# K's transposing load by rows of one key, and a score matmul that reads with a step of four

## The chip, the cores and the metric

The kernel runs on one core of one Trainium2 chip. The metric is the device time of one execution in microseconds. The five engines of a core work from their own instruction streams and meet at semaphores: TensorE (PE) multiplies matrices into PSUM, VectorE (DVE), ScalarE (ACT) and GpSimd (POOL) work element by element, and SyncE (SP) issues most of the transfers, which run on 16 DMA engines.

## The reference

Two problems, A and B, of the same sizes are computed independently; their outputs are joined on the last axis. Each is attention against a given cache, between a query and an output projection:

```
B, Sq, D = 16, 80, 576;  Hq, Hkv, Sk, Dh = 32, 16, 512, 128      (bfloat16)
q = (x @ wq).reshape(B, Sq, Hq, Dh).transpose(0, 2, 1, 3)
k, v = k_cache, v_cache, each of the 16 heads used by two query heads
scores = einsum("bhqd,bhkd->bhqk", q, k) * Dh ** -0.5
p = softmax(scores)
o = einsum("bhqk,bhkd->bhqd", p, v)
out = o.transpose(0, 2, 1, 3).reshape(B, Sq, Hq * Dh) @ wo
```

k_cache and v_cache have the shape (16, 16, 512, 128): for one batch row, four heads of K are 2048 keys of 128 numbers, 512 KB that lie in one piece in HBM.

## The kernel before

**Units.** The work is cut into 128 units, 64 of each problem. A unit is one batch row and four K/V heads (a "quad"), with the eight query heads that use them. Each K/V head has 2 x 80 = 160 query rows. 128 of them make one score tile; the 32 left over of each of the four heads are put together in one further tile of 128 rows. So a unit has five score tiles of 128 rows by 512 keys.

**K's load** (`em_ldk`, line 612) is a DMA transpose issued by SP. It brings the unit's 2048 keys into `kT`, with the 128 numbers of a key across the 128 partitions. `kT` has five buffers (`NK`), each of 4 x 512 elements per partition. The source is seen as 512 rows of four consecutive keys, "(g p) j d" with j = 4; in `kT` an element stands at [d, j, g*128 + p]. So `kT[:, ks, j, :]` holds, for each of the four heads, every fourth key.

**V's load** (`em_ldv`, line 616) is a plain DMA that puts four consecutive keys of a head into one partition: partition p has keys 4p to 4p + 3. That is why a score tile must have its columns in the order "j, then p": the four blocks of 128 columns, transposed, then meet the right rows of V.

**Scores.** `em_qk` (line 658) makes the tile of one head by one matmul: the head's queries are the stationary operand, 128 x 128, and K the moving one, `kT[:, ks, :, gl*128:(gl+1)*128]`, four runs of 128 elements, 512 columns in all. `em_qkr` (line 644) makes the left-over tile by four narrow matmuls with 32 query rows each, at the column tiles 0, 32, 64 and 96 of the array; from the third unit on, two units are done in one call, so eight matmuls stand together.

**After the scores**, for each tile: DVE takes the negated maximum (line 667), ACT the exponential with the row sum (line 671), DVE the reciprocal (line 677), POOL multiplies (line 680), PE transposes the tile in four blocks (line 686) and DVE copies them to `pT` (lines 692 and 694). In 45 of the units the left-over tile is transposed by a DMA from SP instead (line 698). Four matmuls for each head multiply with V (line 731); ACT copies the result to `oT` (line 747).

**Projections.** The query projection (line 540, in pieces of 480 and 160 columns) and the output projection (line 781, 288 columns) are spread between the units' work on PE. Query results are moved by ACT or DVE (lines 551 and 552); outputs are stored by SP (line 815). For problem B, x is brought in by four transposing loads: line 481 (640 rows of four blocks of 128 elements) and line 485 (640 rows of one such block).

**The order of the work.** A planner in Python (`_Sched`) gets every operation with a due time, an estimated duration and its resources, and writes out one fixed order for each engine; PSUM banks are given out there too. Score tiles are due 10 tiles before the rest of their unit (`LA`), K's load a further 8 (`KK`). The planner's costs for a K load (`dur=3.4` on SP, `cost=KC` on the DMA) are constants. Each engine runs its list strictly in order, with waits on semaphores; a K load waits until PE has done the score matmuls that read the same buffer five units before, and everything after it on SP waits with it.

Of the kernel before, what the change touches and what calls it, by code (L numbers as in the profile page):

```python
# [73 lines left out]
def _mm(n, cols):  # L74
    return n * (cols * MM1 + MM0)
# [248 lines left out]
def bass_concat_heads__gqa_block_cached__gqa_block_cached__near_ridge_kernel(  # L324
# [27 lines left out]
    with ExitStack() as es:  # L352
# [6 lines left out]
        kT = sb("kT", [128, NK, 4, 512], BF16)  # L359
# [24 lines left out]
        def R(res, ver):  # L384
            return (res, ver)
# [47 lines left out]
        def unit(g):  # L433
            prob, r = divmod(g, NOCT * NPP)
            pair, r = divmod(r, 2 * NPP)
            half, q = divmod(r, 2)
            return prob, 2 * pair + q, half
# [57 lines left out]
        for goct in range(NG):  # L495
            prob, q, half = unit(goct)
# [106 lines left out]
        for U in range(NSU):  # L603
            goct, bl = divmod(U, 8)
            prob, q, half = unit(goct)
            b = half * 8 + bl
            _, kc_ap, vc_ap, _, _ = probs[prob]
            ks, vs, pts, qsl = U % NK, U % NV, U % NPT, goct % NQ

            def em_ldk(e, kc_ap=kc_ap, b=b, q=q, ks=ks):  # L610
                src = kc_ap[b, 4 * q:4 * q + 4, :, :].rearrange("g (p j) d -> (g p) j d", j=4)
                return e.dma_start_transpose(kT[:, ks, :, :], src)

            def em_ldv(e, vc_ap=vc_ap, b=b, q=q, vs=vs):
                src = vc_ap[b, 4 * q:4 * q + 4, :, :].rearrange("g (p j) d -> p g (j d)", j=4)
                return e.dma_start(v_sb[:, vs, :, :], src)

            S.add("sp", 5.0 * gfirst[U] + 0.5 * (U - gfirst[U]) - LA - KK, em_ldk, writes=[R(("kT", ks), U)],
                  dsem="d_k%d" % ks, name="ldk%d" % U, stream="K", dur=3.4, cost=KC)
            S.add("sp", 5.0 * U - VK, em_ldv, writes=[R(("V", vs), U)],  # L620
# [4 lines left out]
            for k in range(5):  # L625
# [5 lines left out]
                gl = k - 1  # L631
# [5 lines left out]
                if k == 0:  # L637
                    group.append((U, vb, ks, qsl, bl, goct))
                    if len(group) == gsize[U]:
                        def em_qkr(e, group=tuple(group)):  # L640
                            last = None
                            for _, vb_, ks_, qsl_, bl_, _ in group:
                                for g4 in range(4):
                                    last = e.matmul(ps[32 * g4:32 * g4 + 32, vb_.phys, :],  # L644
                                                    lhsT=qT[:, qsl_, bl_, g4 * 160 + 128:g4 * 160 + 160],
                                                    rhs=kT[:, ks_, :, g4 * 128:(g4 + 1) * 128],
                                                    start=True, stop=True, tile_position=(0, 32 * g4))
                            return last

                        S.add("pe", Qof[(group[0][0], 0)] - LA + 0.0, em_qkr,  # L650
                              reads=[R(("qT", g_[3], g_[4], i), g_[5]) for g_ in group for i in (1, 3, 5, 7)]
                              + [R(("kT", g_[2]), g_[0]) for g_ in group],
                              writes=[R(g_[1], 0) for g_ in group], name="qkr%d" % U, stream="S",
                              dur=len(group) * (_mm(1, 512) + 0.0105), lat=0.2, alloc=[g_[1] for g_ in group], mode=1)
                        group = []
                else:
                    def em_qk(e, gl=gl, vb=vb, ks=ks, qsl=qsl, bl=bl):
                        return e.matmul(ps[:, vb.phys, :], lhsT=qT[:, qsl, bl, gl * 160:gl * 160 + 128],  # L658
                                        rhs=kT[:, ks, :, gl * 128:(gl + 1) * 128], start=True, stop=True)

                    S.add("pe", tq, em_qk,
                          reads=[R(("qT", qsl, bl, 2 * gl), goct), R(("qT", qsl, bl, 2 * gl + 1), goct),
                                 R(("kT", ks), U)],
                          writes=[R(vb, 0)], name="qk%d" % T, stream="S", dur=_mm(1, 512), lat=0.2, alloc=[vb])
# [230 lines left out]
```

## Time and profile before

| | |
|---|---|
| time, median of 3 runs | 781.7 us (779.27 to 785.27) |
| profiled execution: time / span | 780.9 us / 779.2 us |
| granted TensorE clock | 1.00 |
| busy: PE / DVE / ACT / POOL | 99% / 87% / 78% / 55% |
| DMA: moved, mean rate | 166.44 MB, 214 GB/s |
| DMA packets, of them under 512 B | 386,564, 300,576 |
| K load, time from issue to landing (min/median/max) | 4.3 / 6.0 / 10.6 us |

The profile comes from one execution. The span is the time from the first to the last instruction. "Busy" is the time in which an engine had an instruction running; matmuls are pipelined and their ends are modelled, so PE's busy share is no measure of how fast it works, and the spacing of two matmuls in the chain is more telling than the duration of one. L612 means line 612 of the kernel. "PEld" is the loading of stationary operands, "SPq" the instruction queue of SP. In the lists of waits each line has the waiting engine and line, what it waited for, the total in us, the number of times and the longest. The chain is followed back from the last instruction: at each step to what released it or, if nothing did, to the instruction before it on its engine.

### The profile page before, as it was taken

What the parts mean: (1) busy time and instruction counts of PE and PEld (TensorE: products, weight loads), DVE (VectorE), ACT (ScalarE), POOL (GpSimd) and SP (SyncE); (2) the same over time, 40 slices, a digit from 0 to 9 for tenths busy, and PEclk for the clock granted to TensorE, in tenths of its full rate; (3) what the DMA queues carried; (4) which work ended last, traced back from release to release, by engine and by line L of the source; (5) the groups of instructions that cost most, each with busy time, mean ns of one, the idle gap of its engine ahead of it and who ended that gap; (6) DMA issues with size and microseconds to landing.
All of it is one profiled execution on the core that took longest, in us unless ns stands there. A gap on an engine that the chain in (4) does not pass through costs nothing.

```text
span 779.2 us, 21256 instructions
## 1 busy us (share of the span) xinstructions
PE 772.0 (99%) x8078; PEld 567.5 (73%) x8078; DVE 678.6 (87%) x1558; ACT 611.6 (78%) x1736; POOL 432.4 (55%) x647
## 2 busy tenths in 40 slices
PE   9999999999999999999999999999999999999998
PEld 5576677777777777767777777777777777777786
DVE  4999988888888899888898899988888888989982
ACT  1878988888888888867787777978888887887860
POOL 1555755565655656555655655655655655664660
PEclk9999999999999999999999999999999999999999
DMA  9999999988899999999999999999999978999951
GB/s 249 226 259 240 249 222 247 203 188 197 205 200 213 204 237 247 251 213 227 211 229 214 177 214 244 258 218 237 221 230 202 200 177 196 257 220 210 187 134 32
DMA packets 386564, 166.44 MB, mean 214 GB/s; under 512 B 300576, under 2 KB 383008, under 8 KB 386464
## 3 DMA queue, kind: packets, MB, share of 16 engines
q1 hardware_dynamic: 385248, 163.91, 95.7%
q8 instruction: 65, 1.06, 0.6%
q10 hardware_dynamic: 1216, 1.18, 0.5%
q14 instruction: 35, 0.29, 0.1%
HBM read 87.46 MB, written 2.95 MB: 116 GB/s over the span
## 4 chain that ended last, share of the span: by engine, by line
PE 91%; DVE 7%; DMA 1%; ACT 0%; POOL 0%; issue 0%; SPq 0%
PE ps L540 20%; PE ps L781 20%; PE ps L731 17%; PE ps L686 15%; PE ps L658 13%; DVE negmax L667 4%; PE ps L644 4%; DVE pT L694 2%; DVE qT L552 1%; DMA kT<-in_A_k_cache_dram 1%; PE ps L409 0%; PE ps L464 0%; DVE pT L692 0%; ACT p_sb L671 0%; PE ps L424 0%; POOL p_sb L680 0%
## 5 line engine op out<-in xcount | busy, mean ns | idle before, releaser
L680 POOL TENSOR_SCALAR p_sb<-p_sb,rinv 128x512 bf16<-128x512 bf16 x640 | 430.0, 692 | 325.5 <-DVE rinv L677 325.1
L671 ACT ACTIVATE p_sb<-ps,negmax 128x512 bf16<-128x512 f32 x640 | 441.3, 693 | 84.0 <-DVE negmax L667 77.1
L667 DVE TENSOR_REDUCE negmax<-ps 128x1 f32<-128x512 f32 x640 | 427.8, 679 | 9.6 <-PE ps L658 5.1
L686 PE MATMUL ps<-ident,p_sb 128*128 128x128 bf16 x2380 | 229.7, 219 | 1.1 <-POOL p_sb L680 0.5
L694 DVE COPY pT<-ps 128x512 bf16<-128x512 bf16 x512 | 209.9, 413 | 16.4 <-PE ps L686 14.2
L731 PE MATMUL ps<-pT,v_sb 128*128 128x160 bf16 x2048 | 222.6, 233 | 0.1
L540 PE MATMUL ps<-xT,wq_sb 128*128 128x480 bf16 (+1 forms) x1280 | 213.2, 300 | 0.1
L731 PEld LDWEIGHTS ps<-pT,v_sb 128*128 128x128 bf16 x2048 | 158.4, 98 | 54.3 <-ACT oT L747 5.9
L686 PEld LDWEIGHTS ps<-ident,p_sb 128*128 128x128 bf16 x2380 | 168.7, 98 | 35.7 <-DVE pT L694 6.5
L658 PE MATMUL ps<-kT,qT 128*128 128x512 bf16 x512 | 189.0, 379 | 0.6 <-ACT p_sb L671 0.6
L781 PE MATMUL ps<-wo_sb,oT 128*128 128x288 bf16 x1280 | 171.5, 286 | 0.0
L540 PEld LDWEIGHTS ps<-xT,wq_sb 128*128 128x128 bf16 x1280 | 106.9, 98 | 61.4 <-ACT oT L747 2.6
L781 PEld LDWEIGHTS ps<-wo_sb,oT 128*128 128x128 bf16 x1280 | 122.8, 98 | 34.8 <-ACT qT L551 1.3
L747 ACT CAST oT<-ps 128x320 bf16<-128x320 f32 x256 | 108.7, 425 | 37.0 <-PE ps L731 36.6
L671 ACT ACTIVATION_READ_ACCUMULATOR p_sb<-ps,negmax 128x1 f32 x640 | 130.1, 203 | 0.0
L551 ACT ACTIVATE qT<-ps 128x160 bf16<-128x160 f32 (+1 forms) x159 | 63.2, 398 | 25.9 <-PE ps L540 24.9
L552 DVE TENSOR_SCALAR qT<-ps 128x480 bf16<-128x480 f32 (+1 forms) x97 | 54.7, 564 | 22.2 <-PE ps L540 21.1
L658 PEld LDWEIGHTS ps<-kT,qT 128*128 128x128 bf16 x512 | 49.2, 98 | 6.3 <-ACT p_sb L671 3.1
L809 DVE TENSOR_TENSOR osb<-ps,acc 128x288 bf16<-128x288 f32 x40 | 18.2, 456 | 27.6 <-PE ps L781 27.4
L644 PE MATMUL ps<-kT,qT 128*32 128x512 bf16 x512 | 39.6, 384 | 1.1 <-DMA kT<-in_A_k_cache_dram 0.9
L677 DVE RECIPROCAL rinv<-rowsum 128x1 f32<-128x1 f32 (+1 forms) x173 | 29.6, 171 | 11.1 <-ACT p_sb L671 11.1
L692 DVE COPY pT<-ps 128x512 bf16<-128x512 bf16 x83 | 34.5, 416 | 4.9 <-PE ps L686 4.7
(19 smaller groups left out, 47.0 us busy)
## 6 DMA issues: line engine op xcount, KB each, us to landing
v_sb<-in_A_v_cache_dram SPq DMA_DIRECT2D x64, 512.0 KB, 4.6
v_sb<-in_B_v_cache_dram SPq DMA_DIRECT2D x64, 512.0 KB, 4.6
wo_sb<-in_A_wo_dram SPq DMA_DIRECT2D x8, 576.0 KB, 7.6
wo_sb<-in_B_wo_dram SPq DMA_DIRECT2D x8, 576.0 KB, 7.4
wq_sb<-in_B_wq_dram SPq DMA_DIRECT2D x4, 1024.0 KB, 6.7
out_dram<-osb SPq DMA_DIRECT2D x40, 72.0 KB, 2.3
wq_sb<-in_A_wq_dram SPq DMA_DIRECT2D x2, 1024.0 KB, 7.4
wq_sb<-in_A_wq_dram ACTq DMA_DIRECT2D x2, 512.0 KB, 6.9
```

Of the source, the lines that this page charges most:

```text
L540: last = e.matmul(ps[:, vb.phys, 0:n1 - n0], lhsT=wq_sb[:, wsl, ck, i * 128:(i + 1) * 128], rhs=xT[:, half, ck, n0:n1], start=(ck == 0), s ...
L551: return e.activation(dst, src, AF.Identity, scale=SCALE)
L644: last = e.matmul(ps[32 * g4:32 * g4 + 32, vb_.phys, :], lhsT=qT[:, qsl_, bl_, g4 * 160 + 128:g4 * 160 + 160], rhs=kT[:, ks_, :, g4 * 128: ...
L658: return e.matmul(ps[:, vb.phys, :], lhsT=qT[:, qsl, bl, gl * 160:gl * 160 + 128], rhs=kT[:, ks, :, gl * 128:(gl + 1) * 128], start=True, ...
L667: return e.tensor_reduce(negmax[:, si:si + 1], ps[:, vb.phys, :], axis=AX.X, op=AluOpType.max, negate=True)
L671: return e.activation(p_sb[:, psl, :], ps[:, vb.phys, :], AF.Exp, bias=negmax[:, si:si + 1], scale=1.0, accum_out=rowsum[:, ss, k:k + 1])
L680: return e.tensor_scalar(p_sb[:, psl, :], p_sb[:, psl, :], rinv[:, ss, k:k + 1], 1.0, op0=AluOpType.mult, op1=AluOpType.mult)
L686: last = e.transpose(psb[:, vt.phys, j * 128:(j + 1) * 128], p_sb[:, psl, j * 128:(j + 1) * 128], ident[:])
L694: return e.tensor_copy(pT[:, pts, :, 0:4, gl * 32:gl * 32 + 32], psb[:, vt.phys, 0:512].rearrange("p (j h c) -> p j h c", j=4, h=4))
L731: last = e.matmul(ps[:, vo.phys, off:off + 160], lhsT=v_sb[:, vs, gl, j * 128:(j + 1) * 128], rhs=pT[:, pts, j, :, gl * 32:gl * 32 + 32], ...
L747: return e.copy(dst, src)
L781: last = e.matmul(ps[:, vb.phys, 0:DC], lhsT=oT[:, hi, rb * 128:(rb + 1) * 128], rhs=wo_sb[:, wi, c3 * DC:(c3 + 1) * DC], start=(hi == 0), ...
```

## The change

The load sees the same source as 2048 rows of one key and writes it as one matrix of 128 x 2048. In `kT` the keys of a head now stand in their own order, `kT[:, ks, g, key]`. The score matmuls therefore pick their columns by a step: for j = 0 to 3, the keys j, j + 4, j + 8 and so on, 128 of each. The order of the columns in the score tile is what it was.

```diff
             def em_ldk(e, kc_ap=kc_ap, b=b, q=q, ks=ks):
-                src = kc_ap[b, 4 * q:4 * q + 4, :, :].rearrange("g (p j) d -> (g p) j d", j=4)
-                return e.dma_start_transpose(kT[:, ks, :, :], src)
+                src = kc_ap[b, 4 * q:4 * q + 4, :, :].rearrange("g s d -> (g s) d")
+                return e.dma_start_transpose(kT[:, ks, :, :].rearrange("d g s -> d (g s)"), src)
...
                                     last = e.matmul(ps[32 * g4:32 * g4 + 32, vb_.phys, :],
                                                     lhsT=qT[:, qsl_, bl_, g4 * 160 + 128:g4 * 160 + 160],
-                                                    rhs=kT[:, ks_, :, g4 * 128:(g4 + 1) * 128],
+                                                    rhs=kT[:, ks_, g4, :].rearrange("d (p j) -> d j p", j=4),
                                                     start=True, stop=True, tile_position=(0, 32 * g4))
...
                     def em_qk(e, gl=gl, vb=vb, ks=ks, qsl=qsl, bl=bl):
                         return e.matmul(ps[:, vb.phys, :], lhsT=qT[:, qsl, bl, gl * 160:gl * 160 + 128],
-                                        rhs=kT[:, ks, :, gl * 128:(gl + 1) * 128], start=True, stop=True)
+                                        rhs=kT[:, ks, gl, :].rearrange("d (p j) -> d j p", j=4),
+                                        start=True, stop=True)
```

## The prediction

> **What bounds the kernel now.** I read the page first: busy times, the chain that ended last, the groups; then the chain in order of time inside the steady part, PE's and SP's waits, and the transposing loads by line. Busy times and chain come first.
>
> ```profile
> span 779.2 us, 21256 instructions
> PE 772.0 (99%) x8078; PEld 567.5 (73%) x8078; DVE 678.6 (87%) x1558; ACT 611.6 (78%) x1736; POOL 432.4 (55%) x647
> ...
> q1 hardware_dynamic: 385248, 163.91, 95.7%
> ...
> PE 91%; DVE 7%; DMA 1%; ACT 0%; POOL 0%; issue 0%; SPq 0%
> ```
>
> PE's busy time is modelled, so its 99% alone proves little; but the chain runs 91% in PE and 7% in DVE. The load queue holds the DMA engines for 95.7% of the span, so there are two near-full resources, and I must see whether PE ever waits for the second. PE's list of waits:
>
> ```profile
> PE ps L644 <- DMA kT<-in_A_k_cache_dram: 0.9, 1, 0.9
> PE ps L658 <- ACT p_sb L671: 0.6, 2, 0.3
> ```
>
> One wait for a K load, 0.9 us, at the start; none for V. SP, on the other hand, waits before the K load at L612 for PE to release a kT buffer (134.8 us behind L731, 115.2 behind L686, 115.1 behind L658, and less behind three more lines). So loads are late because PE is late, not the reverse: PE is the bound. The chain in order of time, between 300 and 320 us (start, us, what):
>
> ```profile
> 300.74 0.55 PE ps L644 x8
> ...
> 302.74 0.22 PE ps L658
> 302.95 0.22 PE ps L686 x4
> ...
> 312.23 0.43 PE ps L658 x2
> ```
>
> PE goes from one piece to the next without a gap. A score matmul of 512 columns takes 0.215 us there (0.43 for two); its 379 ns in the groups is a latency, not a spacing. Eight narrow ones (L644: two units, four column tiles each) take 0.55 us, hardly more than two wide ones, so four of them stream at one time.
>
> **The change part by part.**
>
> *1. The load at L612.* It removes 512 source rows of four 256-byte blocks, and adds 2048 rows of one block; the destination is the same 4 KB per partition. Two bounds for the time that SP spends on it come from the other two transposing loads of HBM data, both of 640 rows (duration min/median/max, ns):
>
> ```profile
> L481 SPq DMA_TRANSPOSE xT<-in_B_x_dram x2: 4065/4878/5692, 224.8 to 326.1; - x2
> L485 SPq DMA_TRANSPOSE xT<-in_B_x_dram x2: 1192/1192/1193, 249.3 to 350.8; - x2
> L612 SPq DMA_TRANSPOSE kT<-in_A_k_cache_dram x64: 1721/3684/8411, 2.9 to 361.7; - x64
> ```
>
> L481 has four blocks in a row, L485 one. If a row had a price, the two would cost the same; instead 1920 more blocks cost 4065 - 1192 = 2873 ns, 1.5 ns a block, with about 0.24 us fixed. For 2048 blocks that is 3.3 us, near the 3.68 us of the old form. The other end, a price by the row, would be 4 x 3.68 = 14.7 us a load, 1886 us in all; L485 excludes it. I take no change of SP's time. A rise of a microsecond would be hidden too: the queue behind the K load (V loads, P transposes at L698, output stores) has SP's waits at L612 as slack, 478 us over 128 loads, 3.7 us each.
>
> *2. The transfer itself.* Blocks stay 256 bytes and as many (128 x 2048 of the 300,576 packets under 512 B). Now the blocks of a row lie together and rows are 1 KB apart; after, all 2048 lie one behind the other. No row shows the engines' time for either order alone, so it is bounded: a gain, at most the 0.9 us wait at the start, since PE waits for nothing else of it; a loss only if the queue passes PE, which is the second rival. I take zero.
>
> *3. The order of the keys.* A score row still has its columns in the order (key mod 4, key div 4): before, the load made it, now the matmul's read does. So maxima, exponentials, transposes, V and the output are the same instructions, in the same order, with the same waits. Nothing is moved past a queue.
>
> *4. The read with a step.* Both score matmuls (L644, L658) now take every fourth element of a 1 KB key row, four times over, so their moving operand steps 8 bytes. Streamed columns stay 512, but the read walks 4 x 1024 = 4096 bytes per partition in place of 1024. No operand here is read with a step between elements, so the price has to be bounded.
> - Below: nothing. The output and V matmuls bear only on breaks in a run: L731 reads runs of 32 elements and takes 0.28 us for four matmuls of 160 columns, 0.43 ns a column, as L658 takes 0.42. And four L644 streams together read 4 x 1024 bytes in one slot of about 0.22 us plus their start, so the memory as a whole can deliver what one stepped stream asks for. A gain has no source: the column rate is already that of every other matmul.
> - Above: four times. The fastest single stream in the trace is 1024 bytes in 0.215 us, 4.8 bytes/ns; POOL reads the same operand shape in 692 ns (1.5 bytes/ns). If a stream can walk no faster than that, 4096 bytes take 0.86 us.
> - Which value: neither end has a row of its own. The total of L644 speaks for spare capacity in the memory, not in one stream; stepped, L644 asks for four times that total. I take the middle in ratio, **twice the time**, an estimate: 0.215 us more for each wide matmul and for each set of four narrow ones.
>
> The sum: 512 wide matmuls x 0.215 = 110.1 us; 128 sets x 0.215 = 27.5 us; together 137.6 us of PE time. In the 91% of the chain that is PE it stands in full; in the 7% that runs over DVE PE had room, and I let the added time vanish there: 0.93 x 137.6 = 128 us. What hides it otherwise? Nothing: PE has no other slack. What is late next: DVE, ACT and POOL get longer idle times, SP waits longer for kT buffers, and the DMA share falls to about 0.957 x 779/907 = 82%. The profiled execution took 780.9 us (span 779.2 and 1.7 around it), 0.8 below the median 781.7. **780.9 + 128 = 909 us**, +16%.
>
> The Trainium skill, page "Advanced Engine Details and Errata", section "SBUF Cachelines", speaks against this: SBUF has 16-byte lines, a reader keeps full speed while it uses a line at least twice, and a step of 8 bytes does just that; by it part 4 would cost nothing and the sum would be 781. No row here shows a stepped read, so the trace neither agrees nor disagrees.
>
> **The rivals.**
> - *The step is free.* A matmul reads at 0.215 us as before, because a stream has a reserve of four that contiguous reads never use. For it: the four streams of L644 at once show SBUF delivering this much. Against it: one stream never showed it, PE draws an element each 0.42 ns where POOL takes 1.35, and stepped L644 sets ask for 16 times one stream. Then parts 1 to 4 are all zero: **781 us** (776 to 788), not slower. The page's rule named above gives this case.
> - *The queue becomes the bound.* The step is free, but contiguous blocks queue up on one place in HBM, or the 16 engines lose the overlap that rows 1 KB apart gave. q1 holds 95.7% of the engines, 746 us; K is 67 of its 164 MB (41%) by bytes and 262,144 of 385,248 packets (68%). At 1.25 times the time per K packet the queue needs 76 to 127 us more, 822 to 873 us against PE's 781: it decides from about 7 to 12% slower K packets, as 746 us has some 35 us to spare to PE's bound. **845 us**. Against it: L485's blocks each start a new row and its SP time shows no price for that.
> - *Only the narrow ones pay.* If the limit is the memory's total, which one L644 set already reaches, a wide stepped matmul just fits and a stepped set of four takes four slots: 128 x 3 x 0.215 = 82.6 us, x 0.93 = 77: **858 us**. A smaller fixed loss per element on both kinds would also land between 795 and 880.
> - *One stream at its present rate is the limit.* Then all score matmuls take four slots, 3 x 137.6 = 413 us: near **1190 us**.
> - *The load gets faster.* PE's wait of 0.9 us goes, and a start a little earlier: **779 us**. More than 1% (8 us) would need PE to find gaps that the chain doesn't show. The Trainium skill, page "DMA: Bandwidth & Descriptors", section "Latency and other measured facts", gives 261 GB/s for transposes with a non-contiguous middle dimension and 350 to 400 for contiguous ones; by that K's transfer shortens, and the time by this rival's 1 or 2 us.
>
> That the change doesn't do what it says is no rival of weight: source, destination and read pattern are all spelled out in the two expressions.
>
> **How the numbers follow.** Twice the time 0.38; free 0.24; the queue 0.11; narrow ones only or a smaller loss 0.13; four times 0.08; faster by over 1% 0.06. Slower by over 1% is 0.38 + 0.11 + 0.13 + 0.08 = 0.70; within 1% (about what a measurement here can tell from no change) 0.24; faster 0.06. The range runs from the free case to just above the forecast, which gets 918.5 if DVE's 7% hides nothing: 776 to 925. It leaves out four times and faster, 0.14. The forecast's own range is 895 to 925.
>
> **What would show it.** In the changed profile: L658 in the chain at 0.43 us and 0.86 for two, L644 x8 near 0.98; at 0.22 and 0.55 the step is free, and then any loss must show as PE waiting for kT. L612 should keep 3.3 to 3.7 us on SP, and q1 its 385,248 packets: fewer packets or a much lower share would mean that contiguous blocks are joined. Matmuls at lines 540, 686, 731 and 781 keep their spacing. A price strictly per row in L612 (near 14 us), or score matmuls at any ratio but two, makes the forecast wrong.

## The result and the profile after

The changed kernel takes 923.6 us (923.37 to 924.07 in 4 runs), against 782.5 us for the kernel before in the same comparison: 1.181 times the time, 95% interval 1.178 to 1.184. The forecast was 909 us, with a range of 776 to 925. The granted TensorE clock was 1.00 in both.

Busy times, load queue and chain of the changed kernel (below line 658 its line numbers are one higher: 686 became 687, 731 became 732):

```profile
span 922.0 us, 21256 instructions
PE 917.4 (100%) x8078; PEld 577.7 (63%) x8078; DVE 704.2 (76%) x1558; ACT 625.4 (68%) x1736; POOL 432.7 (47%) x647
...
q1 hardware_dynamic: 385248, 163.91, 79.8%
...
PE 99%; DMA 1%; ACT 0%; SPq 0%; DVE 0%; issue 0%
PE ps L658 25%; PE ps L540 19%; PE ps L782 17%; PE ps L732 16%; PE ps L687 14%; PE ps L644 7%; DMA acc<-in_A_x_dram 1%; PE ps L464 0%; ACT p_sb L672 0%; SPq L449 0%; DVE osb L810 0%; ACT qT L551 0%
```

Read the PE entry first: 145.4 us more busy time (917.4 against 772.0), a little more than the 142.8 us by which the span grew. PE's time that was not busy went from 7.2 us to 4.6. Packets and bytes of the load queue are unchanged, and its share fell because the span is longer. The chain now runs in PE alone; the 7% that went over DVE are gone. The chain in order of time between 350 and 375 us (start, us, what) shows which matmuls grew:

```profile
351.52 0.45 PE ps L658
351.97 0.23 PE ps L687 x4
352.20 0.90 PE ps L658 x2
...
355.11 1.03 PE ps L644 x8
```

L658 went from 0.22 us to 0.45, L644's eight from 0.55 to 1.03; the four transposes between them kept their 0.22 or 0.23. The same lines as durations, with the transposing load (min/median/max, ns):

```profile
L658 PE MATMUL ps<-kT,qT x512: 608/612/632, 18.1 to 893.6; 128*128 128x512 bf16 x171
L612 SPq DMA_TRANSPOSE kT<-in_A_k_cache_dram x64: 1236/3279/8027, 3.3 to 417.9; - x64
```

L658's duration was 379 ns before. L612, whose four-block form took 3684 ns, is not longer.

### The profile page after: what moved, and what is told of

It is laid out like the page before. It is cut to its first block, busy times and chain, and to the rows that moved or that the text cites. A ratio compares the mean times of both kernels' runs of the same rounds, so it can differ in the third digit from the quotient of the medians.

```text
span 922.0 us, 21256 instructions
## 1 busy us (share of the span) xinstructions
PE 917.4 (100%) x8078; PEld 577.7 (63%) x8078; DVE 704.2 (76%) x1558; ACT 625.4 (68%) x1736; POOL 432.7 (47%) x647
## 3 DMA queue, kind: packets, MB, share of 16 engines
q1 hardware_dynamic: 385248, 163.91, 79.8%
## 4 chain that ended last, share of the span: by engine, by line
PE 99%; DMA 1%; ACT 0%; SPq 0%; DVE 0%; issue 0%
PE ps L658 25%; PE ps L540 19%; PE ps L782 17%; PE ps L732 16%; PE ps L687 14%; PE ps L644 7%; DMA acc<-in_A_x_dram 1%; PE ps L464 0%; ACT p_sb L672 0%; SPq L449 0%; DVE osb L810 0%; ACT qT L551 0%
## 5 line engine op out<-in xcount | busy, mean ns | idle before, releaser
L658 PE MATMUL ps<-kT,qT 128*128 128x512 bf16 x512 | 307.7, 613 | 0.1
L732 PEld LDWEIGHTS ps<-pT,v_sb 128*128 128x128 bf16 x2048 | 164.7, 99 | 124.2 <-issue 85.1
L732 PE MATMUL ps<-pT,v_sb 128*128 128x160 bf16 x2048 | 226.9, 234 | 0.0
L687 PEld LDWEIGHTS ps<-ident,p_sb 128*128 128x128 bf16 x2380 | 173.3, 98 | 58.2 <-issue 34.3
L540 PEld LDWEIGHTS ps<-xT,wq_sb 128*128 128x128 bf16 x1280 | 110.3, 99 | 91.4 <-issue 37.5
L644 PE MATMUL ps<-kT,qT 128*32 128x512 bf16 x512 | 69.9, 626 | 0.0
L658 PEld LDWEIGHTS ps<-kT,qT 128*128 128x128 bf16 x512 | 48.6, 98 | 5.0 <-issue 2.7
```

What stands on the lines that cost most here:

```text
L540: last = e.matmul(ps[:, vb.phys, 0:n1 - n0], lhsT=wq_sb[:, wsl, ck, i * 128:(i + 1) * 128], rhs=xT[:, half, ck, n0:n1], start=(ck == 0), s ...
L644: last = e.matmul(ps[32 * g4:32 * g4 + 32, vb_.phys, :], lhsT=qT[:, qsl_, bl_, g4 * 160 + 128:g4 * 160 + 160], rhs=kT[:, ks_, g4, :].rearr ...
L687: last = e.transpose(psb[:, vt.phys, j * 128:(j + 1) * 128], p_sb[:, psl, j * 128:(j + 1) * 128], ident[:])
L732: last = e.matmul(ps[:, vo.phys, off:off + 160], lhsT=v_sb[:, vs, gl, j * 128:(j + 1) * 128], rhs=pT[:, pts, j, :, gl * 32:gl * 32 + 32], ...
```

## The experiments

### The load alone, and the read alone

The change has two parts that can be separated if the columns of the scores need not meet the right rows of V: such a kernel does the same work, but its result is no longer the reference's. The first kernel has the new load and reads without a step:

```diff
-rhs=kT[:, ks, gl, :].rearrange("d (p j) -> d j p", j=4)
+rhs=kT[:, ks, gl, :]
```

and the same at L644.

> The new load (2048 rows of one key), but both score matmuls read the 512 keys of a head in one contiguous run; so the columns of the scores stand in another order than V's rows, which no longer belong together. My theory: the load has no price and the step has all of it, so this gives 780 us (776 to 785), L658 at 0.215 us in the chain, L612 at 3.3 to 3.7 us on SP. Rival, the load costs part of it: over 790 us, with waits of PE for kT. Rival, the contiguous load is faster and PE profits: under 776 us.

Measured: 780.07 us, 0.9995 times the kernel before (0.9984 to 1.0006). The load in this kernel:

```profile
L612 SPq DMA_TRANSPOSE kT<-in_A_k_cache_dram x64: 1721/3577/8242, 3.3 to 359.9; - x64
L612 SPq DMA_TRANSPOSE kT<-in_B_k_cache_dram x64: 1769/3494/7804, 364.0 to 730.0; - x64
...
DMA to landing us min/median/max: 4.3/5.9/10.4
```

2048 rows of one block take SP 3.5 us, as 512 rows of four did (3.7), and land after 5.9 us in place of 6.0. So the load costs no time and brings none, and both rivals that hung on it fall for this change.

The second kernel is the other half, the old load under the stepped read (L644 steps likewise):

```diff
-rhs=kT[:, ks, :, gl * 128:(gl + 1) * 128]
+rhs=kT[:, ks, gl, :].rearrange("d (p j) -> d j p", j=4)
```

> The old load (512 rows of four keys), with the stepped read over what it brings: the scores then belong to other keys than in the reference. My theory: the whole loss is the step, so 920 us (915 to 928), L658 at 0.43 to 0.45 us. Rival, part of the loss belongs to the load: clearly under 915 us.

Measured: 923.75 us, 1.183 times (1.181 to 1.185), with L658 at 612 ns again. The step alone has the whole loss.

### Which property of the step has the price

"Twice" was a middle between two bounds, not a mechanism. The next four kernels change only the pattern of the read, in both score matmuls and again without regard to the rows of V: the form `"d (p j) -> d j p"` with another j, or pairs:

```diff
-rearrange("d (p j) -> d j p", j=4)
+rearrange("d (p j) -> d j p", j=2)               # step 2; likewise j=8 and j=16
...
+rearrange("d (p a b) -> d a p b", a=4, b=2)      # pairs, 8 elements from pair to pair
```

> As the changed kernel, but the read steps by two elements (4 bytes), so that the columns of the scores stand in another order than V's rows. Theory W, a stream gets 4 bytes, two neighbouring elements, in the time of two columns, and with a step one of them is lost: L658 again 0.43 us, the whole again 920 us. Theory B, a stream walks at most about 9.6 bytes/ns (or one 16-byte line in 1.7 ns): 2048 bytes fit in 0.215 us, and the time is 780 us.

> As the changed kernel, but the read steps by eight elements (16 bytes); column order again not V's. Theory W (one element of each 4-byte pair is used, whatever the step): L658 0.43 us, 920 us. Theory B (bytes or lines walked): 8192 bytes, four times the contiguous slot: L658 0.86 us, near 1200 us.

> As the changed kernel, but the read takes pairs of neighbouring elements, 8 elements from pair to pair, in four passes (column order not V's). It walks 4096 bytes like the step of four, and touches as many 16-byte lines (256 for each matmul) with two elements from each, but has half as many jumps. Theory L, a stream fetches one 16-byte line in about 1.7 ns, whatever is used of it: L658 0.43 us again, 920 us. Rival J, each jump has a price: 256 jumps in place of 512, L658 0.22 to 0.33 us, 780 to 850 us.

> As the changed kernel, but with a step of 16 elements (32 bytes; column order not V's). Theory L: each of the 512 columns has a 16-byte line of its own as with a step of eight, so L658 stays at 0.88 us and the whole near 1210 us. Rival, the price is by the bytes walked (or by wider lines): 16,384 bytes, L658 about 1.75 us and the whole near 1770 us.

Measured: 784.7 us with a step of two (1.0047 times, 1.003 to 1.006), 1213 us with eight, 1221 us with sixteen, 923.6 us with the pairs; the last three are single runs. L658's durations, first in the kernel before, then in this order:

```profile
L658 PE MATMUL ps<-kT,qT x512: 379/379/390, 17.5 to 751.0; 128*128 128x512 bf16 x171
```

```profile
L658 PE MATMUL ps<-kT,qT x512: 385/388/401, 18.2 to 754.7; 128*128 128x512 bf16 x171
```

```profile
L658 PE MATMUL ps<-kT,qT x512: 1058/1060/1080, 18.7 to 1182.5; 128*128 128x512 bf16 x171
```

```profile
L658 PE MATMUL ps<-kT,qT x512: 1075/1077/1097, 18.5 to 1190.4; 128*128 128x512 bf16 x171
```

```profile
L658 PE MATMUL ps<-kT,qT x512: 608/612/632, 17.9 to 893.4; 128*128 128x512 bf16 x171
```

Count the 16-byte pieces of a partition that one matmul has to fetch. A pass over the 1024 bytes of a head touches 64 of them, so a step of two (two passes) needs 128, four 256, eight 512; with sixteen each pass touches only every second piece, and sixteen passes need 512 again. The pairs make four passes of 64: 256.

| read | pieces of 16 bytes | L658, median ns |
|---|---|---|
| contiguous | 64 | 379 |
| step 2 | 128 | 388 |
| step 4 | 256 | 612 |
| pairs, 8 apart | 256 | 612 |
| step 8 | 512 | 1060 |
| step 16 | 512 | 1077 |

From 256 to 512 pieces the duration grows by 1060 - 612 = 448 ns, 1.75 ns a piece. Taken back from 612, that leaves 612 - 256 x 1.75 = 164 ns that don't depend on the read; the contiguous read leaves the same, 379 - 215 = 164. For 128 pieces the two give 164 + 224 = 388 ns, what was measured; for 64 they give 276, less than the 379 ns that the 512 columns take by themselves. So a stream needs about 1.75 ns for each new 16-byte piece, whatever it takes from it, and a column 0.42 ns; the longer of the two decides. The times of the kernels bear this out: spread over the 640 slots (512 wide matmuls and 128 sets of four), the steps of two, four and eight cost 6, 223 and 676 ns a slot, where the rule gives 9, 233 and 681. The pairs settle it against a price by the jump (half as many jumps, the same 612 ns), the step of two against "any step halves", the step of sixteen against a price by the bytes walked: twice the way of a step of eight for 17 ns more. Pieces of 8 bytes would make a step of four cost what one of eight does, and pieces of 32 bytes would leave one of eight well under one of sixteen; neither is so. What the 17 ns are stays open.

### The narrow matmuls, and how much of a small loss arrives

Here only L644 steps; L658 reads a contiguous run.

```diff
 # em_qk
-rhs=kT[:, ks, gl, :].rearrange("d (p j) -> d j p", j=4)
+rhs=kT[:, ks, gl, :]
```

> As the changed kernel, but only the narrow matmuls at L644 step; those at L658 read a contiguous run (column order not V's for these tiles). Theory P, each stream has its own port: a set of four takes 0.21 to 0.24 us more, 128 x 0.23 = 30 us, and as PE is the bound all of it lands: 810 us. If the 7% of the chain that ran over DVE hid its share: 808 us. Rival, four streams share one limit: three slots more for a set, 83 us, so 863 us.

Measured: 808.7 us, 1.036 times (1.034 to 1.038). That is 28.0 us more than the 780.7 of its comparison, 26.8 to 29.5 by the interval, 0.219 us for each of the 128 sets. The chain of this kernel:

```profile
350.18 1.03 PE ps L644 x8
...
364.32 0.22 PE ps L658
```

Two sets of four take 1.03 us, nearly twice their own 0.55 and not four times: four streams at once each have the rate of one. The rest of the loss, 923.6 - 808.7 = 114.9 us, is 0.224 us for each of the 512 wide matmuls. Whether the 7% over DVE hid anything is too fine for this run: 30 x 0.93 = 27.9 and the undiscounted 0.215 x 128 = 27.5 both lie in the interval.

### The step moved to where it is cheap

The PE transposes at the changed kernel's line 687 have the exponentials as their stationary operand. If the scores keep the natural order of the keys, the transposes can take every fourth column, and the transposed blocks meet V's rows as before. The 45 left-over tiles that go through a DMA transpose keep a stepped score read:

```diff
 # em_qkr, rd_ true for the 45 units
+rhs=kk.rearrange("d (p j) -> d j p", j=4) if rd_ else kk
...
 # em_tr
-p_sb[:, psl, j * 128:(j + 1) * 128], ident[:])
+p_sb[:, psl, :].rearrange("p (q j) -> p j q", j=4)[:, j, :], ident[:])
```

> The new load; the score matmuls read contiguous runs, and the step of four is moved to the PE transposes at L687 (line 687 of the changed kernel), whose stationary operand takes every fourth column of the exponentials; only the 45 left-over tiles that a DMA transposes keep a stepped score read. By theory L a stationary load of 128 columns with a step of 8 bytes touches 64 lines, 0.11 us, about what it takes now (98 ns) beside the matmuls: then 45 x 0.23 = 10 us are left, 791 us. Rival, a stepped stationary operand costs twice its 98 ns and the weight loads of 2380 transposes stand out against their 56 ns spacing: up to 2380 x 0.1 = 238 us, so up to 1030 us.

Measured: 790.2 us, 1.0125 times (1.011 to 1.014), so 9.6 us, the 45 stepped sets (45 x 0.219 = 9.9). The weight load of the transposes in the kernel before, then weight load and matmul in this one (now L688):

```profile
L686 PEld LDWEIGHTS ps<-ident,p_sb x2380: 95/98/99, 25.2 to 761.6; 128*128 128x128 bf16 x199
...
L688 PEld LDWEIGHTS ps<-ident,p_sb x2380: 109/113/138, 25.8 to 771.2; 128*128 128x128 bf16 x199
L688 PE MATMUL ps<-ident,p_sb x2380: 217/220/250, 25.8 to 771.3; 128*128 128x128 bf16 x199
```

A stepped stationary load takes 113 ns in place of 98. It touches 128 x 8 = 1024 bytes, 64 pieces, 64 x 1.75 = 112 ns; that fits the price of a moving read, but it is one point and doesn't prove it. The 15 ns are real, but these loads run beside other matmuls, and 2380 of them don't show in the time.

The last 45 can be relieved too, if ScalarE picks every fourth score when it makes the exponentials of those tiles:

```diff
 # em_exp, for the 45 tiles
+dst = dst.rearrange("p (j q) -> p j q", j=4)
+src = src.rearrange("p (q j) -> p j q", j=4)
```

> As the kernel with the step in the stationary operand of the PE transposes, but the 45 left-over tiles that a DMA transposes are also scored by contiguous reads; for these ScalarE's exponential picks every fourth score from PSUM. Theory: PE has no stepped moving read left, so 780 to 782 us, the time of before. ScalarE may take up to twice its 0.69 us for these 45 tiles, 31 us in all, which its idle fifth hides. Rival: the longer exponentials hold up the DMA transposes behind them, 785 to 800 us.

Measured: 780.5 us, 1.0006 times (0.9996 to 1.0016): the new load and no loss, but no gain either. The exponentials took 694 ns on the mean, 693 before, so the stepped 45 cost ScalarE next to nothing: 1 ns on the mean of 640 would be 14 ns for each of them. No kernel here is faster than the one before, and the load alone says why: there was nothing to win.

### A fuller load queue

The prediction's second rival needed slower K transfers, which the change did not bring. The next kernel gives the queue more work in another way: scores in natural order by contiguous reads, and V loaded to match, one key of 256 bytes for each partition and block.

```diff
-src = vc_ap[b, 4 * q:4 * q + 4, :, :].rearrange("g (p j) d -> p g (j d)", j=4)
-return e.dma_start(v_sb[:, vs, :, :], src)
+src = vc_ap[b, 4 * q:4 * q + 4, :, :].rearrange("g s d -> (g s) d")
+return e.dma_start(v_sb[:, vs, :, :].rearrange("p g (j d) -> p (g j) d", j=4),
+                   src.rearrange("(k p) d -> p k d", p=128))
```

> The new load and contiguous score reads, so the scores have the keys in their natural order; V is loaded to match, with blocks of 128 keys across the partitions: 2048 pieces of 256 bytes in place of 512 of 1 KB for each unit. This gives the load queue more to do while PE is as before, which is what the prediction's queue rival needed. If the queue is near its limit at 93 to 96%: four packets of 256 bytes at 18 ns take 72 ns for the 46 ns of one of 1 KB, 57% more for V's 41% of the bytes, some 118% of the span, 880 to 920 us, with PE waiting for kT and v_sb. If the share counts mostly packets that wait, and there is real slack: 780 to 800 us.

Measured: 823.5 us, 1.057 times (1.053 to 1.061), between the two forecasts. Its busy times, queue and chain:

```profile
PE 781.3 (95%) x8078; PEld 571.5 (70%) x8078; DVE 680.9 (83%) x1558; ACT 612.7 (75%) x1736; POOL 432.5 (53%) x647
...
q1 hardware_dynamic: 581856, 163.91, 106.0%
...
PE 80%; DVE 9%; ACT 4%; DMA 4%; issue 2%; SPq 0%; POOL 0%; DVEq 0%
```

and PE's longest waits in it (L645 are the narrow score matmuls, L733 those with V, L783 the output projection):

```profile
PE ps L645 <- issue: 11.8, 2, 6.8
PE ps L733 <- issue: 4.3, 3, 3.4
PE ps L783 <- DMA wo_sb<-in_B_wo_dram: 4.3, 1, 4.3
```

PE is busy 95% where it was 99%, and transfers are in the chain with 4%. A share of 106% can't be a hold on the engines: packets overlap, and the share adds their times. In the kernel before, the DMA share was already 1.03 between 200 and 600 us, while PE had hardly a gap. So the 95.7% of before was not a queue 4% from its end, yet half as many packets again made PE wait.

The two long waits before the score matmuls have no releaser in the list ("issue"), but the landings in the trace name it. The K loads issued at 92.90 and 318.14 us held SP for 6.5 and 7.5 us, and landed at 101.44 and 327.68; the matmuls started at 101.53 and 327.77. So PE waited for K: what the second rival expected of slower packets came here from more of them.

Not all of the 43 us are waiting. The granted clock of this kernel was 0.981 to 0.988 in its four runs, against 1.00 before. In the trace it was half for 3.4 or 6.8 us at a time, four times, each time beginning within one of PE's four longest pauses (3.4 to 6.8 us); right after the two waits for K, eight narrow matmuls took 1.04 and 1.05 us in place of 0.55. PE's busy time grew by 9.3 us (781.3 against 772.0), and its time not busy by 31.2 (38.4 against 7.2). So some 9 us of the loss go with the clock and some 31 with the pauses (an estimate from these two differences).

## Why the prediction was right, and where it was off

**PE as the bound:** right. The loss arrived as PE time, all but 2.6 of 145.4 us, the load's form changed nothing, and SP still waits for PE before K's loads.

**Part 1, the load's time on SP:** 3.3 us by blocks, against 14.7 by rows; measured 3.5 us with the load alone. A row has no price of its own, as the comparison of L481 with L485 said. That the size came out is luck: the 2048 blocks are no fixed 3.3 us. The shortest load of the changed kernel held SP for 1.24 us, little more than the 1.19 of L485's 640 blocks, and with the step of eight, where the queue's share was 58.2%, the medians were 2.5 and 2.2 us:

```profile
L612 SPq DMA_TRANSPOSE kT<-in_A_k_cache_dram x64: 1236/2480/7899, 3.2 to 552.4; - x64
L612 SPq DMA_TRANSPOSE kT<-in_B_k_cache_dram x64: 1236/2188/5613, 559.1 to 1143.7; - x64
```

The time was shorter where the queue's share was lower; what holds SP beyond the 1.24 us is not shown.

**Part 2, the transfer:** taken at zero, and zero within 0.2%. The rule cited from the Trainium skill, page "DMA: Bandwidth & Descriptors", section "Latency and other measured facts" (faster transposes from a contiguous source), doesn't show here: K lands after 5.9 us in place of 6.0. Whether the old load is the slower case that the page means, no run here shows.

**Part 4, the step:** the value chosen, twice, was right, and that was luck: it was the middle in ratio between two bounds, with no mechanism behind it. The bounds were one and four times, and four is indeed the price where every element has a 16-byte piece of its own (1213 us, forecast 1190 for that rival). But "bytes walked per ns" is not the limit, as the step of sixteen shows. It is pieces of 16 bytes: a step of four uses two elements of each, and 2 x 0.42 ns is half of 1.75 ns.

The rule that spoke against the forecast (the Trainium skill, page "Advanced Engine Details and Errata", section "SBUF Cachelines") is right about the unit of 16 bytes and wrong here about the count. Two uses of a line are not enough for a matmul's moving operand at the full clock (612 against 379 ns in duration, 0.45 against 0.22 us in the chain); four, as with the step of two, nearly are (388 ns). "The step is free" was thus nearly true for a step of two elements and false for four.

**The sum:** this is what was off, by some 15 us; the time lies near the upper end of the forecast's own 895 to 925. The factor 0.93, which let 9.6 us vanish where the chain ran over DVE, was wrong: the chain of the changed kernel is 99% PE, and 142.8 us of span came from 137.6 us of estimated PE time. A chain that passes through DVE doesn't mean that PE was idle there; PE had only 779.2 - 772.0 = 7.2 us not busy in all. With the load alone, at the same 780 us, the chain had 15% in DVE, so that share isn't even a steady property of the kernel. Without the factor the forecast was 918.5 us. The remaining 5 us are the size of the added time: 0.224 us for a wide matmul and 0.219 for a set, not 0.215.

**The narrow ones only:** fell; four streams don't share a limit that a step of four reaches. **The DMA share** was put at 82%, and came out at 79.8%.

## What to carry to other kernels

Before a matmul's moving operand gets a step, count the 16-byte pieces that each partition must fetch, and compare 1.75 ns for each with 0.42 ns for each column (measured for bf16 and 512 columns at a granted clock of 1.00): with 2-byte elements and 512 columns a step of two costs next to nothing, four doubles a matmul's slot, eight or sixteen quadruples it. If an order of elements has to be changed on the way, put the step where the engine has time beside the bound: in a stationary operand whose load is hidden, or in an exponential on ScalarE. And the part of a chain that runs over another engine is no measure of the idle time of the one that is full; read that from its busy time or its waits.

## What was new about the hardware

- A matmul's moving read took 1.75 ns for each new 16-byte piece of a partition, and four column tiles did this at one time without loss to one another (0.219 us more for a set of four, 0.224 for one wide matmul).
- A stationary load with a step of four took 113 ns in place of 98, which fits the same price (64 pieces, 112 ns) without proving it.
- ScalarE's read of every fourth fp32 value from PSUM had no price that shows (mean 694 against 693 ns, with 45 of 640 stepped).
- The share of the DMA engines' time that packets take can pass 100% (106.0%), so 95.7% was not yet the end of the queue's capacity.
- SP's time for one and the same transposing load went with the queue's share: 1.24 us at the least, in the median 3.3 and 3.1 us at a queue share of 79.8% and 2.5 and 2.2 at 58.2%.
- In the kernel with the fuller queue, the granted clock fell to half within each of PE's four pauses of 3.4 us or more, and eight narrow matmuls right behind two of them took 1.04 and 1.05 us in place of 0.55.
